# A decode step on one core: the first weight transfer issued as two, 16 partitions and then 112

## The chip, the core and the metric

The kernel runs on one core of a Trainium2 chip. The metric is device time in microseconds (us) for one launch, from the first instruction to the end of the last one. Before the change three timed runs gave 1314.3, 1315.67 and 1316.89 us, so the median is 1315.67 us. The engines are named as in the profile: PE multiplies matrices, DVE works on vectors, ACT on activations, POOL does a few small things at the start, and SP issues nearly all the transfers from HBM (the memory of the chip) to SBUF (the memory of the core, 128 partitions).

## What is computed

One decoding step of a transformer block for two sequences (B = 2), one token each, D = 512, 32 heads of 128, a cache of 8192 positions, and a feed-forward layer of width 1792, all in float32:

```python
def _A_ref(x, k_cache, v_cache, wq, wo):
    q = (x @ wq).reshape(B, 1, 32, 128).transpose(0, 2, 1, 3)
    scores = einsum("bhqd,bhkd->bhqk", q, k_cache) * (128 ** -0.5)
    p = softmax(scores)
    o = einsum("bhqk,bhkd->bhqd", p, v_cache)
    return o.transpose(0, 2, 1, 3).reshape(B, 1, 4096) @ wo

h  = x + _A_ref(layernorm(x), k_cache, v_cache, wq, wo)
h2 = h + (silu(layernorm(h) @ w_gate) * (layernorm(h) @ w_up)) @ w_down
```

The two caches are 2 x 32 x 8192 x 128 floats each, 268.4 MB apiece. The weight `wq` is 512 x 4096 floats, 8.39 MB. Every byte is used once.

## The kernel before, in words

SBUF holds three large areas of 64 KB per partition, A, B and C. Keys of the units alternate between A (`kA`) and B (`kB`). The values (`vC`) always go to C, and so do `wq` at the very start (`wqC`) and the last weight, `w_down` (`wdC`), at the end. A unit is two heads of one sequence: 128 partitions by 16384 floats, 8.39 MB of keys and as much of values. There are 32 units.

All large loads pass through the helper `load` (line 131), which issues one transfer on SP and lets it add 16 to a semaphore when it has landed. SP issues them in the order of the program, and the transfers of SP form one queue (q1 in the profile) on the core's 16 DMA engines. The order at the start is `wq`, the keys of unit 0 in two halves (`k0`, `k0b`), the keys of unit 1 (`kB`), then the values of unit 0. Before the values SP waits until the matmuls that read `wq` are done, since both lie in area C:

```python
if u == 0:
    sp.wait_ge(s["pe"].h, 3)
else:
    sp.wait_ge(s["pv"].h, u)
```

From there on SP issues the values of unit u when PE is through with those of the unit before, and the keys of unit u+2 when DVE has summed up those of unit u (`red`).

`wq` is laid out so that partition p holds rows 4p to 4p+3 of the matrix, which is one contiguous piece of 64 KB in HBM per partition. The input `x` comes by a small transfer of its own on ACT's queue. While `wq` is on its way DVE, POOL and PE normalize `x` and turn it (`xT`). PE then waits for `wq` and for `xT` (the two waits ahead of line 256), multiplies (line 261), ACT copies the result (line 270), PE spreads it over the partitions (line 281), and ACT writes `q_all` (line 291). With the first piece of `q_all` and `k0`, DVE begins the scores of unit 0: products (line 302) and sums (line 308).

For each unit DVE then takes the maximum (337, 340), PE and ACT do the softmax (393 to 401, 352 to 356), PE multiplies with the values (408) in a loop, and the output is gathered (371, 420). After the last unit come the output projection, the second normalization and the feed-forward layer, whose last load is `wdC`; lines 535 to 569 work on it, and the result is written by two small transfers.

Of the kernel before, what the change touches and what calls it, by code (L numbers as in the profile page):

```python
# [9 lines left out]
P = 128  # L10
# [35 lines left out]
def decode_block(nc, x, k_cache, v_cache, wq, wo, w_gate, w_up, w_down, out):  # L46
# [10 lines left out]
    sp, pe, act, dve, pool = nc.sync, nc.tensor, nc.scalar, nc.vector, nc.gpsimd  # L57

    def arena(name, at, shape):
        return nc.alloc_sbuf_tensor_at(name, list(shape), F32, offset=at)  # L60
# [4 lines left out]
    wq_s = arena("wqC", C, [P, DC, H * DH])  # L65
# [5 lines left out]
    m = Map(nc, BASE + 3 * SLOT, nc.sbuf_usable_end)  # L71
# [46 lines left out]
    s = {n: Count(nc, f"s_{n}") for n in names}  # L118
# [11 lines left out]
    def load(c, dst, src):  # L130
        c.on(sp.dma_start(dst, src), 16)
# [4 lines left out]
    flat = lambda t, a, b: t[:, a:b, :].rearrange("p j d -> p (j d)")  # L136

    s["x"].on(act.dma_start(xs[:, :], x.rearrange("b s d -> (b s) d")), 16)
    load(s["wq"], wq_s[:, :, :], wq.rearrange("(p c) m -> p c m", p=P))
    half = NJ // 2  # L140
    for name, j0 in (("k0", 0), ("k0b", half)):
        load(
# [108 lines left out]
    sel_done = s["dve"].n  # L251


    pe.wait_ge(s["wq"].h, 16)
    pe.wait_ge(s["dve"].h, xT_done)
    rows = (wide0, wide1)
    for r in range(2):
# [380 lines left out]
```

## Time and profile before

| | |
|---|---|
| median of three runs | 1315.67 us |
| time of the profiled execution | 1314.05 us |
| its span, first to last instruction | 1312.3 us |
| DVE busy | 1130.5 us, 86% |
| PE busy | 425.3 us, 32% |
| bytes read from HBM | 564.66 MB |
| queue q1, share of the 16 DMA engines' time | 99.4% |

The span is what the page's shares refer to; the profiled execution took 1.75 us more than it, which is what lies around it. The share of a queue is the time that its packets took, summed over the 16 DMA engines, over 16 times the span. In the views by windows a packet is counted whole where it starts, so windows of a few microseconds scatter.

### The profile page before, as it was taken

The numbers are of one execution on the slowest core, as the hardware profiler recorded it, in microseconds if no ns is written. First come the engines' busy times: TensorE is split into PE (matmuls) and PEld (weight loads), VectorE is DVE, ScalarE is ACT, GpSimd is POOL, SyncE is SP. The second block draws the span as 40 slices with busy tenths as digits, with TensorE's granted clock in tenths as the row PEclk, the third lists the DMA queues.
The fourth block names the chain that finished last, engine by engine and source line by source line (L and its number), as shares of the span: only waits on it lengthen the run. The fifth ranks groups of instructions, "written<-read, shape, count | busy, mean of one in ns | idle before, by whom it ended". The sixth has DMA issues, their size and how long they took to land. (4 is left out here: it accounts for less than half of the span.)

```text
span 1312.3 us, 6527 instructions
## 1 busy us (share of the span) xinstructions
PE 425.3 (32%) x2844; PEld 142.8 (11%) x2844; DVE 1130.5 (86%) x191; ACT 75.7 (6%) x242; POOL 1.8 (0%) x8
## 2 busy tenths in 40 slices
PE   3233223332322333322333332233332123333267
PEld 0110001110001111000111000011100011101012
DVE  1999998889888889988888998888898888899831
ACT  0100000000000000000000000000000000000010
POOL 0000000000000000000000000000000000000000
PEclk9665566666556666655666655666665566665578
DMA  9999999999999999999999999999999999999997
GB/s 408 450 422 443 419 443 419 443 440 427 439 423 443 431 435 439 423 441 421 445 439 425 439 423 443 437 429 440 423 441 427 439 442 423 439 423 439 443 419 313
DMA packets 10540, 564.77 MB, mean 430 GB/s; under 512 B 1178, under 2 KB 1186, under 8 KB 1444
## 3 DMA queue, kind: packets, MB, share of 16 engines
q1 hardware_dynamic: 10520, 564.66, 99.4%
q8 instruction: 4, 0.07, 0.0%
q14 instruction: 4, 0.03, 0.0%
q10 hardware_dynamic: 12, 0.01, 0.0%
HBM read 564.66 MB, written 0.00 MB: 430 GB/s over the span
## 5 line engine op out<-in xcount | busy, mean ns | idle before, releaser
L408 PE MATMUL bank<-vC,p 128*8 128x512 f32 x2048 | 291.8, 734 | 584.9 <-PEq L121 584.9
L302 DVE TENSOR_TENSOR kA<-kA,q_all 128x16384 f32<-128x16384 f32 (+1 forms) x17 | 275.7, 16220 | 64.3 <-DMA kA<-in_A_k_cache_dram 36.9
L302 DVE TENSOR_TENSOR kB<-kB,q_all 128x16384 f32<-128x16384 f32 x16 | 275.6, 17223 | 39.6 <-DMA kB<-in_A_k_cache_dram 39.6
L308 DVE TENSOR_REDUCE s<-kA 128x128 f32<-128x16384 f32 (+1 forms) x17 | 275.7, 16216 | 0.1
L308 DVE TENSOR_REDUCE s<-kB 128x128 f32<-128x16384 f32 x16 | 275.5, 17220 | 0.0
L408 PEld LDWEIGHTS bank<-vC,p 128*8 128x8 f32 x2048 | 60.5, 103 | 790.1 <-issue 790.1
L393 PE MATMUL bank<-ident,m 128*1 128x128 f32 x64 | 18.7, 395 | 182.9 <-PEq L121 182.9
L371 ACT ACTIVATE osb<-bank,r 128x512 f32<-128x512 f32 x32 | 22.0, 687 | 902.0 <-PE bank L408 902.0
L420 PE MATMUL bank<-sel,osb 128*128 128x2 f32 x256 | 32.8, 250 | 29.0 <-PEq L121 29.0
L420 PEld LDWEIGHTS bank<-sel,osb 128*128 128x128 f32 x256 | 31.0, 191 | 57.7 <-issue 57.7
L401 PE MATMUL bank<-rs,hm 128*128 128x1 f32 x64 | 17.9, 348 | 44.1 <-PEq L121 44.1
L340 DVE TENSOR_REDUCE gm<-bank 1x2 f32<-1x128 f32 x32 | 8.9, 278 | 24.6 <-PE bank L393 24.6
L356 ACT ACTIVATE p<-s,nb 64x128 f32<-64x128 f32 x64 | 25.9, 405 | 1.4
L199 DVE BATCH_NORM_STATS2 stats<-bank 2x6 f32<-2x512 f32 x1 | 0.7, 686 | 28.7 <-PE bank L460 28.7
L393 PEld LDWEIGHTS bank<-ident,m 128*1 128x1 f32 x64 | 3.6, 80 | 185.1 <-issue 185.1
L397 PE MATMUL bank<-gm,nscale 1*128 1x2 f32 x64 | 17.6, 343 | 14.8 <-PEq L121 14.8
L401 PEld LDWEIGHTS bank<-rs,hm 128*128 128x128 f32 x64 | 16.1, 312 | 46.0 <-issue 46.0
L397 PEld LDWEIGHTS bank<-gm,nscale 1*128 1x128 f32 x64 | 15.8, 305 | 29.9 <-issue 29.9
L352 ACT ACTIVATE nb<-bank 128x2 f32<-128x2 f32 x32 | 5.5, 172 | 228.2 <-PE bank L397 228.2
L261 PE MATMUL bank<-wqC,xT 128*32 128x512 f32 x64 | 9.1, 732 | 16.4 <-DMA wqC<-in_A_wq_dram 16.4
L356 ACT ACTIVATION_READ_ACCUMULATOR p<-s,nb 64x1 f32 x64 | 11.8, 185 | 0.0
L337 DVE TENSOR_REDUCE m<-s 128x1 f32<-128x128 f32 x32 | 9.2, 286 | 1.1
(71 smaller groups left out, 87.3 us busy)
## 6 DMA issues: line engine op xcount, KB each, us to landing
kA<-in_A_k_cache_dram SPq DMA_DIRECT2D x2, 4096.0 KB, 36.3
vC<-in_A_v_cache_dram SPq DMA_DIRECT2D x1, 6144.0 KB, 24.7
wgB<-in_B_w_gate_dram SPq DMA_DIRECT2D x1, 3584.0 KB, 31.9
wdC<-in_B_w_down_dram SPq DMA_DIRECT2D x1, 3328.0 KB, 20.8
wuB<-in_B_w_up_dram SPq DMA_DIRECT2D x1, 2688.0 KB, 37.9
vC<-in_A_v_cache_dram SPq DMA_DIRECT2D x1, 2048.0 KB, 29.2
wuB<-in_B_w_up_dram SPq DMA_DIRECT2D x1, 896.0 KB, 39.6
vC<-in_A_v_cache_dram SPq DMA_DIRECT2D x31, 29.3
```

The source lines that it names most:

```text
L261: ins = pe.matmul(rows[r][32 * t : 32 * t + 32, :], xT[:, c, :], wq_s[:, c, n0 : n0 + 512], start=(c == 0), stop=(c == DC - 1),)
L302: dve.tensor_tensor(kt, kt, q_all[:, u, :][:, None, :].to_broadcast([P, n, DH]), op=OP.mult)
L308: return dve.tensor_reduce(s_t[:, j0 : j0 + n], ks[u % 2][:, j0 : j0 + n, :], axis=AX.X, op=OP.add)
L337: s["mt"].on(dve.tensor_reduce(m_t[:, :], s_t[:, :], axis=AX.X, op=OP.max))
L340: dve.tensor_reduce(gm[:, :], small1[0:1, :P].rearrange("p (e q) -> p e q", e=2), axis=AX.X, op=OP.max,)
L356: ins = act.activation(p2[a:z, :, e], s_t[a:z, :], AF.Exp, bias=nb[a:z, e : e + 1], scale=SCALE, accum_out=rs[a:z, :],)
L371: act.activation(osb[:, :, :].rearrange("p j d -> p (j d)"), opart[:, :], AF.Copy, scale=r_t[:, :],)
L393: pe.matmul(small1[0:1, :P], m_t[:, :], ident[:, :], start=True, stop=True).then_inc(s["mrow"].h, 1)
L397: pe.matmul(small1[:, 264:266], nscale[:, :], gm[:, :], start=True, stop=True).then_inc(s["nbp"].h, 1)
L401: pe.matmul(small1[:, 256:257], hm[:, :], rs[:, :], start=True, stop=True).then_inc(s["den"].h, 1)
L408: ins = pe.matmul(opart[32 * t : 32 * t + 8, :], p2[:, 4 * g : 4 * g + 4, :].rearrange("p j b -> p (j b)"), vs[:, 4 * g : 4 * g + 4, :].re ...
L420: ins = pe.matmul(small2[:, 16:18], osb[:, j, :], sel8[:, j, :], start=(j == 0), stop=(j == 3))
```

## The change

The transfer of `wq` is issued as two, one behind the other, on the same queue: the first to partitions 0 to 15 (1.05 MB), the second to partitions 16 to 127 (7.34 MB). Both add 16 to the same semaphore, and PE now waits for 32. On both sides the four rows of a partition are named as one run of 16384 floats. Bytes, destination, and everything after it in the program are as they were.

```diff
     s["x"].on(act.dma_start(xs[:, :], x.rearrange("b s d -> (b s) d")), 16)
-    load(s["wq"], wq_s[:, :, :], wq.rearrange("(p c) m -> p c m", p=P))
+    wq_src = wq.rearrange("(p c) m -> p (c m)", p=P)
+    for a, z in ((0, 16), (16, P)):
+        load(s["wq"], wq_s[a:z, :, :].rearrange("p c m -> p (c m)"), wq_src[a:z, :])
     half = NJ // 2
@@
-    pe.wait_ge(s["wq"].h, 16)
+    pe.wait_ge(s["wq"].h, 32)
     pe.wait_ge(s["dve"].h, xT_done)
```

On SP, at the start of the program, the transfers stood in this order before (`wqC` is `wq` in area C, the numbers are partitions by floats):

```order
L131 DMA wqC<-in_A_wq_dram 128x16384
L131 DMA kA<-in_A_k_cache_dram 128x8192 x2
L131 DMA kB<-in_A_k_cache_dram 128x16384
L131 DMA vC<-in_A_v_cache_dram 128x16384
L131 DMA kA<-in_A_k_cache_dram 128x16384
```

They now stand so:

```order
L131 DMA wqC<-in_A_wq_dram 16x16384
L131 DMA wqC<-in_A_wq_dram 112x16384
L131 DMA kA<-in_A_k_cache_dram 128x8192 x2
L131 DMA kB<-in_A_k_cache_dram 128x16384
L131 DMA vC<-in_A_v_cache_dram 128x16384
```

One transfer became two of 16 and 112 partitions; all the others keep their shapes and their order. On PE, DVE, ACT and POOL the rows are the same as before.

## The prediction, made before the changed kernel was run

> **What bounds the kernel now.** I read the page's slices and its queues first, then the chain of waits, then the first 100 us in order of time.
>
> ```profile
> DMA  9999999999999999999999999999999999999997
> q1 hardware_dynamic: 10520, 564.66, 99.4%
> HBM read 564.66 MB, written 0.00 MB: 430 GB/s over the span
> ```
>
> The DMA engines are busy in every slice but the end of the last. DVE with 86% is busy too, but the queue of transfers never runs dry, and the bytes set the time. The queue's row gives the pace of one DMA engine: 564.66 MB / (0.994 x 16 x 1312.3 us) = 27.06 GB/s. So the 64 KB that one partition of `wq` takes occupy one engine for 65,536 B / 27.06 GB/s = 2.42 us. I call this time T and work with it below.
>
> ```profile
> by line: DMA wdC<-in_B_w_down_dram 1.6%; PE bank L408 0.7%; PE bank L535 0.3%; DVE ysb L544 0.0%; PE bank L550 0.0%; issue 0.0%; DVE res L569 0.0%; PE bank L560 0.0%
> ...
> 1284.12 20.79 DMA wdC<-in_B_w_down_dram
> 1304.91 0.14 issue
> 1305.04 3.63 PE bank L535 x52
> ```
>
> The chain of waits ends in the last load, which lands at 1304.91 us, and 7.4 us of computing follow. With every engine full from the start to there, a delay of any one DMA engine at the start is still there at 1304.91 unless something later gives it slack. What could give slack is the moment when the queue is empty. For that I read SP, DVE and PE in order of time:
>
> ```profile
> 0.74 0.39 SPq L131 DMA_DIRECT2D wqC<-in_A_wq_dram  x1
> 1.20 0.89 SPq L131 DMA_DIRECT2D kA<-in_A_k_cache_dram  x2
> 2.12 0.53 SPq L131 DMA_DIRECT2D kB<-in_A_k_cache_dram  x1
> ...
> 6.32 0.17 DVE L229 COPY xT<-bank 128x8 f32<-128x8 f32 x1 [0.73 <-PE bank L222]
> ...
> 22.67 9.10 PE L261 MATMUL bank<-wqC,xT 128*32 128x512 f32 x64 [16.38 <-DMA wqC<-in_A_wq_dram]
> ...
> 31.84 0.33 SPq L131 DMA_DIRECT2D vC<-in_A_v_cache_dram  x1
> ...
> 34.34 8.69 DVE L302 TENSOR_TENSOR kA<-kA,q_all 128x8192 f32<-128x8192 f32 x1 [27.40 <-ACT q_all L291]
> ```
> ```profile
> 69.10 0.33 SPq L131 DMA_DIRECT2D kA<-in_A_k_cache_dram  x1
> ```
>
> `wq` has landed at about 22.6 us. Behind it lie 16.8 MB of keys, 16T = 38.7 us of work, to about 61.3 us. The values of unit 0 are issued at 31.84, 29 us before the queue would need them, and last to about 80.7 us; the next keys are issued at 69.10, 11.6 us ahead. So the stock behind `wq` is never empty. Everything that these issues wait for (the `wq` matmuls, then `q_all`, then DVE's sums of unit 0) itself starts when `wq` lands. Move the landing by d and the issues move by d, and so does the queue: the stock stays what it is, and d reaches the end of the kernel. It isn't used up by idle time, since there is none.
>
> **The change part by part.** First the small parts. *One more issue on SP* is one more row like the 0.39 us one at 0.74. It pushes the issue of the keys from 1.20 to about 1.6 us; cover is the `wq` transfer, which keeps the engines until about 22.6. Cost 0, and 0.4 us if the cover were gone. *The wait for 32* is one instruction as before; it ends when the later of the two transfers has landed. Behind it on PE are the 64 matmuls of line 261, and for these wait ACT, DVE and SP's first values, as just counted. `xT` (6.49 us) is there long before. *The merged dimensions* leave one run of 64 KB per partition: 0.
>
> *An earlier start* would be a gain. The only row that bounds it is the landing of `wq`:
>
> ```profile
> wqC<-in_A_wq_dram SPq DMA_DIRECT2D x1, 21.9
> ```
>
> Of these 21.9 us, 8T = 19.4 us are bytes (128 partitions over 16 engines are 8T each), so at most 2.5 us go to starting and finishing. A first transfer of 16 partitions may get its descriptions to the engines sooner than one of 128. Part of the 2.5 us must be latency that any transfer has: the bounds are 0 and 2.5 us, and I take 0.5, nearer the low end because two issues now stand where one did.
>
> *The split itself* is the large term, and the trace has no row for a big transfer to fewer than 128 partitions. Every large one writes all 128 evenly, so its rows fit two pictures. In picture A the 27.06 GB/s belong to each DMA engine wherever it writes. Then 16 partitions are 1T for each engine, 112 are 7T, and the sum is 8T as before: cost 0. In picture B they belong to places: 128 partitions in 16 groups of 8, each group taking 27.06 GB/s, and engines that meet in a group share it. As long as a transfer covers all groups evenly one can't see the difference. Under B the cost of the first transfer depends on how many groups 16 neighbouring partitions reach. If they reach all 16 it is 1T, if they all lie behind one it is 16T = 38.7 us. Between ends so far apart I take the geometric middle, 4 groups: 4T = 9.7 us, where 1T would have done.
>
> The Trainium skill bears on this. "SBUF — State Buffer", section "Door 1: The DMA port swizzle", says that DMA bandwidth depends on how many of 16 SBUF ports the partitions of a transfer reach, and its table gives partitions 0 to 15 four ports and 104 GB/s at 1 MiB. By that figure the first transfer would be an estimated 10.1 us, and picture A would be out. No run here has shown it so far. "DMA: Bandwidth & Descriptors", section "Rules for kernel authors", also says of two transfers to disjoint partition halves not to bother, and to use one of 128 partitions.
>
> Under B the second transfer costs as well. Each engine has 7 partitions to write, 7T if engines never meet in a group, 14T if each always meets one other. In a transfer of 128 the engines can each have a group to themselves; with 7 neighbours each, cut at partitions 16, 23, 30 and so on, they straddle groups of 4 or 8 and must meet some of the time. I take the middle, 10.5T = 25.4 us. What counts is the slowest engine, not the mean, because the semaphore waits for all of them and because nothing later evens the queue out: engines that got through early run ahead into the keys, and then wait for issues that hang on the slow one.
>
> The sum under B: 4T + 10.5T = 14.5T instead of 8T, so +6.5T = +15.7 us, bounds 4T + 7T - 8T = +3T = +7.3 us and 4T + 14T - 8T = +10T = +24.2 us. Less 0.5 us for the start it is +15.2. The profiled execution's 1314.05 us (span 1312.3 and 1.75 around it) becomes 1329.2 us; it lies 1.62 us below the median of the runs, so the median becomes **1330.8 us**, from 1322.5 to 1339.4 by the bounds.
>
> **The rivals.** *Not slower: the start alone.* If picture A holds, the only thing left is the earlier start. Its place is the 2.5 us between issue and landing that aren't bytes, its price 0 to -2.5 us, and it decides as soon as 16 partitions take the engines no more than 1T + 0.2T. The time is 1313.2 to 1315.7 us, with my 0.5 us 1315.2. For it speaks that no row shows engines sharing anything; against it, that all rows are of the one even shape, so they couldn't show it.
>
> *Much slower: partitions dealt out in turn.* Under B, if engine e gets partitions 16+e, 32+e and so on instead of seven neighbours, all 16 engines are always in 16 neighbouring partitions, and each of the 8 rounds costs 4T instead of 1T: 32T - 8T = +24T = +58.1 us, 1373.3 us less the start. Against it: engines that drift apart would no longer meet, so even then it should come out below that.
>
> *Fewer engines.* Under A, the 112 partitions might go to fewer than 16 engines, with 8 engines 14 each: 1T + 14T - 8T = +7T = +16.9 us, 1332 us. That would look like my forecast in time; the share of the DMA engines in the first 40 us tells them apart, since under B the engines are slow but occupied, and here half of them go ahead to the keys. A split into 14 engines with 8 each would be only +1T, 2.4 us. 7 partitions on each of 16 come out even, so I hold this for unlikely.
>
> **How the numbers follow.** About 0.2% (2.6 us) is what a measurement of this kernel can tell from no change. Chances: picture B with neighbours 0.62, picture A with the start alone 0.20, dealt out in turn 0.08, fewer engines 0.10. I put B over A because any unevenness costs the whole kernel its slowest engine and only perfect independence costs nothing, and because one pace in all slices, for rows of 64 KB, for halves of 32 KB and for weights alike, is what an even share of the places would give as well. All of B, the deal in turn and fewer engines are slower by over 0.2%: 0.80. Of A's 0.20, 0.03 goes to faster, as it takes the whole 2.5 us and a little scatter, and 0.17 to within 0.2%. The likeliest case's own range is 1322.5 to 1339.4. The range for 8 in 10 goes down to 1314.8, into the case of no change, and up to 1341.0, which leaves out the deal in turn and A's best half.
>
> **What would show it.** In the changed profile the 16-partition transfer's time from issue to landing: some 11 to 12 us under B, under 5 us under A. Then the start of the matmuls of line 263 (261 before): 22.67 us before, about 38 us under B, 22 us under A. The first slice's 408 GB/s would fall by the delay's share of 32.8 us, to between 220 and 350, the other slices stay at 420 to 450, and the wait for DVE's first products grows by the same 15 us. The last load lands later by what the matmuls started later. If the matmuls start late and the end doesn't move, there was slack that I haven't seen, and the step from landing to end is wrong. If the first transfer lands early and the second late, the first term is wrong and the second has the cause.

## The result, and the profile after

The changed kernel takes 1334.82 us (median of five runs, 1333.91 to 1336.03) against 1315.67 us (five runs, 1313.74 to 1316.89): a ratio of 1.0154, 95% interval 1.0141 to 1.0166. By the medians it is 19.15 us more for the same bytes (their quotient is 1.0146, inside the interval).

The slices of the page, first GB/s before, then the share of the DMA engines and GB/s after (40 slices, 33.4 us each after):

```profile
GB/s 408 450 422 443 419 443 419 443 440 427 439 423 443 431 435 439 423 441 421 445 439 425 439 423 443 437 429 440 423 441 427 439 442 423 439 423 439 443 419 313
```
```profile
DMA  9999999999999999999999999999999999999996
GB/s 216 376 437 432 426 432 440 440 433 428 432 436 440 432 434 428 434 440 434 432 430 432 440 436 436 430 430 434 440 436 432 428 433 438 438 432 430 432 429 288
```

The loss is in the first two slices. The last slice is lower as well, 288 after 313, because in this profile the computing behind the last load took longer, as shown below. In the row of busy shares the loss can't be seen: the engines show 9 tenths and more while they move 216 GB/s, half of what they moved before.

The packets in the two traces, which the views don't list one by one, show where the time goes. Each partition of `wq` is one packet of 64 KB. Before the change 16 packets were under way at once, as many as there are engines, and each took 2.42 us (up to 3.3 us in the first round). After it the 16 packets of the first transfer run side by side and take 7.7 to 9.1 us each. The 112 of the second follow in 16 rows of seven, one behind the other, and take 2.8 to 6.3 us each, 4.6 us in the median. The share of the DMA engines is 0.97 over the first 45 us, at 222 GB/s: a packet that is held up counts as busy.

The same start in order of time after the change, from the timeline, and the view of the tile `wqC`:

```profile
0.74 0.87 SPq L131 DMA_DIRECT2D wqC<-in_A_wq_dram  x2
1.65 1.11 SPq L131 DMA_DIRECT2D kA<-in_A_k_cache_dram  x2
...
6.32 0.17 DVE L231 COPY xT<-bank 128x8 f32<-128x8 f32 x1 [0.73 <-PE bank L224]
...
44.06 9.71 PE L263 MATMUL bank<-wqC,xT 128*32 128x512 f32 x64 [37.78 <-DMA wqC<-in_A_wq_dram]
...
53.84 0.33 SPq L131 DMA_DIRECT2D vC<-in_A_v_cache_dram  x1
...
56.33 8.69 DVE L304 TENSOR_TENSOR kA<-kA,q_all 128x8192 f32<-128x8192 f32 x1 [49.40 <-ACT q_all L293]
```
```profile
DMA to landing us min/median/max: 12.2/27.5/42.8
```

The 16 partitions land 12.2 us after their issue, the other 112 after 42.8 us, where all 128 had taken 21.9. PE waits 37.78 us for `wq` instead of 16.38, and the matmuls, the issue of the first values and DVE's first products all come 21 to 22 us later (22.67 to 44.06, 31.84 to 53.84, 34.34 to 56.33).

The chain of waits ends in the same load as before:

```profile
1303.69 20.78 DMA wdC<-in_B_w_down_dram
1324.48 0.14 issue
1324.61 5.99 PE bank L537 x52
```

It lands at 1324.48 us, 19.57 us later than before (1304.91). The profiled executions are further apart than that, 1314.05 and 1336.03 us, because the matmuls behind the load took 3.63 us in the one and 5.99 in the other. The windows behind the last load (PE busy, its granted clock after POOL) show why, before and after:

```profile
1304.91:1312.30 7.39, 4.23 (x68) 2.79 (x68) 0.72 (x2) 0.38 (x1) 0.00 (x0) 1.00 0.00 1
```
```profile
1324.48:1334.20 9.72, 6.60 (x68) 3.41 (x68) 0.72 (x2) 0.38 (x1) 0.00 (x0) 0.75 0.00 1
```

The granted clock was 1.00 there in one execution and 0.75 in the other. The change isn't what sets it: of the kernels below, the two that start without a delay (the split by columns and every second partition) have 3.65 and 5.31 us at this place in their profiles, and two that start about as late as the changed kernel (the other order and the halves) 3.65 and 3.63.

### The profile page after: what moved, and what is told of

The parts are those of the page before. It is cut to its first block, busy times and chain, and to the rows that moved or that the text cites. A ratio compares the mean times of both kernels' runs of the same rounds, so it can differ in the third digit from the quotient of the medians.

```text
span 1334.2 us, 6528 instructions
## 1 busy us (share of the span) xinstructions
PE 428.3 (32%) x2844; PEld 143.8 (11%) x2844; DVE 1130.4 (85%) x191; ACT 75.7 (6%) x242; POOL 1.8 (0%) x8
## 5 line engine op out<-in xcount | busy, mean ns | idle before, releaser
L422 PE MATMUL bank<-sel,osb 128*128 128x2 f32 x256 | 32.8, 250 | 28.9 <-PEq L121 28.9
```

The source lines that it names most:

```text
L422: ins = pe.matmul(small2[:, 16:18], osb[:, j, :], sel8[:, j, :], start=(j == 0), stop=(j == 3))
```

## The experiments

The edits of the split by columns, the other order and the two kinds of halves are shown against the changed kernel, the others against the kernel before. Each timed kernel ran 4 or 10 times beside 13 runs of the kernel before, from which the second time in each pair comes. The two kernels of loads alone, which are the kernel before with these loads put ahead of it, ran once each, for their traces.

**The same split by columns.** Two transfers of the same sizes, but each to all 128 partitions.

```diff
-    for a, z in ((0, 16), (16, P)):
-        load(s["wq"], wq_s[a:z, :, :].rearrange("p c m -> p (c m)"), wq_src[a:z, :])
+    wq_dst = wq_s[:, :, :].rearrange("p c m -> p (c m)")
+    for a, z in ((0, 2048), (2048, 16384)):
+        load(s["wq"], wq_dst[:, a:z], wq_src[:, a:z])
```

> wq is again issued as two transfers of 1.05 MB and 7.34 MB, but each goes to all 128 partitions (the first 2048 floats of a partition, then the other 14336). Theory B (partitions share places of one pace): both transfers cover all places evenly, so the cost is gone: 1315.7 us within 2.6, wq matmuls start at about 22.7 us. Rival (it costs to have two transfers, or a short one ahead of a long one): the cost stays, about +19 us, 1335.

Measured: 1314.49 us against 1315.55, ratio 0.9998 (0.9988 to 1.0007). The transfers of this kernel by size, and the start of the matmuls:

```profile
wqC<-in_A_wq_dram SPq DMA_DIRECT2D x1, 7168.0 KB, 21.0
wqC<-in_A_wq_dram SPq DMA_DIRECT2D x1, 1024.0 KB, 4.6
```
```profile
22.24 8.50 PE L264 MATMUL bank<-wqC,xT 128*32 128x512 f32 x64 [15.96 <-DMA wqC<-in_A_wq_dram]
```

1 MB to 128 partitions lands after 4.6 us, to 16 partitions after 12.2. Being two, and being a short one ahead of a long one, costs nothing that these runs can tell. The matmuls even start 0.43 us sooner than before, which is the size of the earlier start that the prediction allowed for, but the kernel as a whole doesn't tell it from no change.

**The delay alone.** `wq` loaded once more ahead of everything, into area B. The keys of unit 1 go to the same area, so SP waits for the extra load before it issues them.

```diff
+    wq_x = arena("wqX", BB, [P, DC, H * DH])
+    load(s["wqx"], wq_x[:, :, :], wq.rearrange("(p c) m -> p c m", p=P))
     load(s["wq"], wq_s[:, :, :], wq.rearrange("(p c) m -> p c m", p=P))
...
+    sp.wait_ge(s["wqx"].h, 16)
     load(s["kB"], flat(ks[1], 0, NJ), kv_src(k_cache, 1))
```

> The kernel before with wq loaded once more ahead of everything, to 128 partitions in area B, as pure delay: 8T = 19.4 us more on every DMA engine. If a delay of the queue at the start reaches the end whole, the kernel takes 1335.1 us (+19.4). If the stock of issued transfers or idle time later takes some of it up, it is less: under +10 us.

Measured: 1334.35 us, ratio 1.0149 (1.0132 to 1.0166), +18.8 us by the medians. In the profile the matmuls of `wq` start 19.53 us later than before, and the matmuls behind the last load (line 535 before, 538 here) 19.37:

```profile
42.20 9.70 PE L264 MATMUL bank<-wqC,xT 128*32 128x512 f32 x64 [35.92 <-DMA wqC<-in_A_wq_dram]
```
```profile
1324.41 3.63 PE bank L538 x52
```

So a delay that is the same on all engines at the start reaches the end whole. This step of the prediction had only been argued; here it is shown for such a delay.

**Ten kinds of loads, alone.** Each load is waited for before the next is issued, so the distance from one row's start to the next, halved, is the time of one.

```diff
...
+    probes = (
+        ("fourNear", 0, 4, 1), ("fourFours", 0, 13, 4), ("fourFar", 0, 97, 32),
+        ("sixteenNear", 0, 16, 1), ("sixteenFours", 0, 61, 4), ("sixteenEights", 0, 121, 8),
+        ("halfNear", 0, 64, 1), ("halfTwos", 0, 127, 2),
+        ("restNear", 16, 128, 1), ("allRows", 0, 128, 1),
+    )
+    for name, a, z, step in probes:
+        t = arena(name, C, [P, DC * H * DH])
+        for _ in range(2):
+            load(s["wqx"], t[a:z:step, :], wq_src[a:z:step, :])
+            sp.wait_ge(s["wqx"].h, s["wqx"].n)
```

> The kernel before with ten kinds of loads ahead of it, each twice and each waited for before the next is issued, 64 KB to a partition, into the same area. T = 2.42 us, and 2.5 us of start and end as with wq before. Theory B with places of four neighbours and four partitions 32 further on: 4 neighbouring partitions (fourNear) 4T + 2.5 = 12.2 us, 4 partitions in steps of 4 (fourFours) 1T + 2.5 = 4.9 us, 4 in steps of 32 (fourFar) 2T + 2.5 = 7.3 us; 16 neighbours 12.2, 16 in steps of 4 or of 8 7.3; 64 neighbours 8T + 2.5 = 21.9; 64 in steps of 2 between 4T and 8T, 12.2 to 21.9; 112 neighbours from partition 16 on 8T at least, as in the changed kernel about 13T + 2.5 = 34; 128 21.9. Rival (the number of partitions sets the pace, or any transfer of other than 128 is slow): the three kinds of 4 alike, the three kinds of 16 alike. Picture A (engines alone): 4 and 16 partitions all 4.9, 64 12.2, 112 19.4, 128 21.9.

SP in order of time (start, time from the first issue to the end of the second):

```profile
0.74 11.79 SPq L131 DMA_DIRECT2D fourNear<-in_A_wq_dram  x2
23.96 5.88 SPq L131 DMA_DIRECT2D fourFours<-in_A_wq_dram  x2
34.41 7.77 SPq L131 DMA_DIRECT2D fourFar<-in_A_wq_dram  x2
48.56 12.01 SPq L131 DMA_DIRECT2D sixteenNear<-in_A_wq_dram  x2
71.87 8.11 SPq L131 DMA_DIRECT2D sixteenFours<-in_A_wq_dram  x2
86.93 8.21 SPq L131 DMA_DIRECT2D sixteenEights<-in_A_wq_dram  x2
102.24 23.58 SPq L131 DMA_DIRECT2D halfNear<-in_A_wq_dram  x2
148.43 13.07 SPq L131 DMA_DIRECT2D halfTwos<-in_A_wq_dram  x2
173.70 33.10 SPq L131 DMA_DIRECT2D restNear<-in_A_wq_dram  x2
239.26 22.31 SPq L131 DMA_DIRECT2D allRows<-in_A_wq_dram  x2
283.06 0.33 SPq L131 DMA_DIRECT2D wqC<-in_A_wq_dram  x1
```

| partitions | us for one | less 2.5 us, in T = 2.42 us | theory B |
|---|---|---|---|
| 4 neighbours | 11.6 | 3.8 | 4 |
| 4, every fourth | 5.2 | 1.1 | 1 |
| 4, every 32nd | 7.1 | 1.9 | 2 |
| 16 neighbours | 11.7 | 3.8 | 4 |
| 16, every fourth | 7.5 | 2.1 | 2 |
| 16, every eighth | 7.7 | 2.1 | 2 |
| 64 neighbours (0 to 63) | 23.1 | 8.5 | 8 |
| 64, every second | 12.6 | 4.2 | 4 to 8 |
| 112 (16 to 127) | 32.8 | 12.5 | 8 or more |
| 128 | 21.9 | 8.0 | 8 |

The three kinds of four move the same 256 KB, and differ only in which partitions they write and, with them, which rows of `wq` they read: 11.6, 5.2 and 7.1 us. Sixteen neighbours take no longer than four. The rival of the number of partitions had the three kinds alike, and picture A had 4 and 16 partitions all at 4.9 us; both fall. The packets agree: four neighbours are four packets at once of 8.1 to 8.9 us each, every fourth partition four packets at once of 2.5 to 3.4 us, and 16 neighbours 16 packets at once of 8.3 to 8.9 us. The layout that fits is four neighbouring partitions to a place, and the four that lie 32 further on in the same place. It is the layout that the Trainium skill gives in "SBUF — State Buffer", section "Door 1: The DMA port swizzle", for its 16 ports. That section of the Trainium skill has 104 GB/s for partitions 0 to 15 at 1 MiB; the 1.05 MB here make 90 GB/s over the whole 11.7 us and 114 GB/s over the 9.2 us without start and end.

That the place is in SBUF and not on the side of HBM is argued, not shown: no run reads the same rows into other partitions. Against HBM speaks the end of the kernel before. If a place were a stretch of 256 KB in HBM, four rows of 64 KB, then pieces of 28 KB to a partition, as `w_gate` has them, would share such stretches in another way, nine to one, and the deal to the engines that is even for `wq` would be uneven for `w_gate`. Yet its 128 packets take 1.06 us each, which is the full pace of 27 GB/s again.

**The other order.** The 112 partitions first.

```diff
-    for a, z in ((0, 16), (16, P)):
+    for a, z in ((16, P), (0, 16)):
```

> The same two transfers in the other order, 112 partitions first and then 16. Theory B: what each transfer costs is set by its partitions, not by its turn, so wq again takes some 17T to land and the kernel comes to 1330 to 1337 us. Rival (the order makes the cost, because a small transfer at the head leaves the engines out of step for the large one): the delay shrinks to that of 16 partitions alone, +7.3 us or less, under 1324 us.

Measured: 1335.74 us, ratio 1.0164 (1.0147 to 1.0181). The matmuls start here:

```profile
44.60 9.49 PE L263 MATMUL bank<-wqC,xT 128*32 128x512 f32 x64 [38.32 <-DMA wqC<-in_A_wq_dram]
```

44.60 us against 44.06 with the 16 first: the turn makes 0.5 us at most, the partitions make the rest.

**Two halves, of neighbours and of every second partition.** Number, sizes and order of the transfers are the same in both kernels.

```diff
-    for a, z in ((0, 16), (16, P)):
+    for a, z in ((0, 64), (64, P)):
```

> wq in two transfers of 64 partitions, 0 to 63 and 64 to 127. In the probe 64 neighbours took 23.1 us each alone, 20.6 us without the 2.5 us of start and end: 8.5T where an even share is 4T. Theory B: 2 x 20.6 = 41.2 us instead of 19.4, so +21.8 at the landing of wq; what overlaps where one ends and the other begins can only lessen it, at most to 8T = +0, since the two halves reach different places: between 1325 and 1337 us. Rival (only an odd count such as 112 or a short first transfer costs): 1315.7.

```diff
-    for a, z in ((0, 16), (16, P)):
-        load(s["wq"], wq_s[a:z, :, :].rearrange("p c m -> p (c m)"), wq_src[a:z, :])
+    wq_dst = wq_s[:, :, :].rearrange("p c m -> p (c m)")
+    for a, z in ((0, 127), (1, 128)):
+        load(s["wq"], wq_dst[a:z:2, :], wq_src[a:z:2, :])
```

> The same as the halves in number, size and order of transfers, but the first takes the 64 even partitions and the second the 64 odd ones. In the probe 64 partitions in steps of 2 took 12.6 us alone, 10.1 without start and end, 4.2T. Theory B: 2 x 4.2T = 8.4T for 8T, +0.8 us, 1316.5 us within 2.6. Rival (64 partitions are slow as such): as slow as the halves.

Measured: the halves 1335.24 us against 1314.45, ratio 1.0170 (1.0139 to 1.0201; three of the four runs lie between 1335.10 and 1335.24, the fourth at 1342.46); every second partition 1316.07 us, ratio 1.0005 (0.9995 to 1.0015). The matmuls, first of the halves, then of every second:

```profile
44.17 8.95 PE L263 MATMUL bank<-wqC,xT 128*32 128x512 f32 x64 [37.88 <-DMA wqC<-in_A_wq_dram]
```
```profile
23.04 8.50 PE L264 MATMUL bank<-wqC,xT 128*32 128x512 f32 x64 [16.76 <-DMA wqC<-in_A_wq_dram]
```

This pair is the plainest: 44.17 or 23.04 us for the same two transfers of 64 partitions, depending on which 64. Behind the first round of 16, the packets of the halves take 4.9 to 5.1 us each, those of every second partition 2.42. The halves' +21.5 us at the matmuls is 2 x 20.6 - 19.4 = 21.8 with almost nothing overlapping. "Don't bother" with disjoint halves, as the Trainium skill has it in "DMA: Bandwidth & Descriptors", section "Rules for kernel authors", holds here: two halves of neighbours cost 21.5 us, and two of every second partition gain nothing. The Trainium skill also says, in "SBUF — State Buffer", section "Can I just issue two DMAs to hit both halves?", that only one transfer spanning all 128 partitions reaches all 16 ports. Read as every partition in one transfer, that doesn't hold here: 64 partitions, every second, moved 4.19 MB in 10.1 us, 415 GB/s, in the probe.

**The 16 partitions alone.** The kernel before, with `wq`'s first 16 partitions loaded once more ahead of it into area B.

```diff
+    wq_x = arena("wqX", BB, [P, DC * H * DH])
+    load(s["wqx"], wq_x[0:16, :], wq.rearrange("(p c) m -> p (c m)", p=P)[0:16, :])
     load(s["wq"], wq_s[:, :, :], wq.rearrange("(p c) m -> p c m", p=P))
...
+    sp.wait_ge(s["wqx"].h, 16)
     load(s["kB"], flat(ks[1], 0, NJ), kv_src(k_cache, 1))
```

> The kernel before with one more transfer ahead of wq: its partitions 0 to 15 (1.05 MB) into area B, as pure delay. Theory B: 4T = 9.7 us (9.2 in the probe) on the engines ahead of an undisturbed wq, so 1325.0 us. Picture A, where only bytes count: 1T = 2.4 us, 1318.0 us.

Measured: 1324.08 us against 1314.45, ratio 1.0065 (1.0048 to 1.0081): +9.6 us by the medians, and 9.3 us at the start of the matmuls in the profile (31.96), for 1 MB that would take 1T = 2.4 us when spread evenly.

```profile
wqX<-in_A_wq_dram SPq DMA_DIRECT2D x1, 12.1
wqC<-in_A_wq_dram SPq DMA_DIRECT2D x1, 30.7
```

**Where the 112's time comes from.** More loads alone, in the same manner.

```diff
...
+    probes = (
+        ("rest", 16, 128), ("restLow", 0, 112), ("ninetysix", 32, 128),
+        ("eighty", 48, 128), ("upperHalf", 64, 128), ("fortyeight", 16, 64),
+    )
```

> More loads alone, 64 KB to a partition, each twice. What of the 12.5T of partitions 16 to 127 is the uneven load on the places (8T, as no place holds more than 8 partitions) and what comes from engines that meet? In time from issue to issue, 2.5 us of it start and end: if it is the load of the fullest place alone, all of 16 to 127, 0 to 111, 32 to 127, 48 to 127 and 64 to 127 take 8T + 2.5 = 21.9 us or a little over, and 16 to 63 too (8 partitions in each of four places). If meeting adds to it because 112 isn't a multiple of 32, then 112 stays at 32 us in both positions, 96 and 64 come to 22 to 23 us, and 80 and 48 lie above their 8T.

```profile
0.74 33.98 SPq L131 DMA_DIRECT2D rest<-in_A_wq_dram  x2
68.09 32.72 SPq L131 DMA_DIRECT2D restLow<-in_A_wq_dram  x2
133.31 32.15 SPq L131 DMA_DIRECT2D ninetysix<-in_A_wq_dram  x2
197.43 27.45 SPq L131 DMA_DIRECT2D eighty<-in_A_wq_dram  x2
251.63 23.32 SPq L131 DMA_DIRECT2D upperHalf<-in_A_wq_dram  x2
297.41 26.77 SPq L131 DMA_DIRECT2D fortyeight<-in_A_wq_dram  x2
350.69 0.35 SPq L131 DMA_DIRECT2D wqC<-in_A_wq_dram  x1
```

Halved, in us: 33.7, 32.6, 32.1, 27.1, 22.9 and 26.6; less 2.5 and in T: 12.9, 12.5, 12.2, 10.2, 8.4 and 10.0. In each of them the fullest place holds 8 partitions, so an uneven load alone would give 8T throughout. Only the half of 64 is near it. The others take 2T to 5T more, and not because 112 isn't a multiple of 32: 96 partitions take 12.2T. That part of the expectation was wrong. The packets point to engines that meet, round after round: the 96 partitions go in six rounds of 16 packets, and behind the first round each packet takes 4.7 to 5.1 us, twice the 2.42 of a packet in the even loads.

A working that fits: let each of 16 engines take its share of neighbouring partitions in order (3, 5, 6 or 7 of them), all in step, and let each step last as long as the fullest place in it. With the layout of the first probe that gives 9T for 16 to 63, 10T for 48 to 127, 12T for 32 to 127 and 14T for the 112, against 10.0, 10.2, 12.2 and 12.5 to 12.9. It doesn't fit 128, or 64 in steps of two, for which it gives 16T and 8T where 8.0 and 4.2 were measured; there the shares must be dealt in another way. The packets confirm the number of rounds (3, 5, 6 and 7), but not which engine wrote which partition, which neither the views nor the packets tell; so this stays a fit and is not shown.

## Why the prediction was right, point by point

**The bound and the way to the end.** Right for a delay that is the same on all engines: the queue is full, and 19.5 us come out as 19.4 at the end. Not quite for the uneven one: in the changed kernel 21.4 us at the matmuls become 19.6 at the last load, so 1.8 us didn't arrive, where the prediction let the delay reach the end whole. The halves lose 0.6 us on this way and the other order 0.8. Both kernels have packets of queue q8 (`instruction`, 16 KB each) on one of the engines. In the packets of the trace before, one of these takes 0.96 us at about 38 us, and from there on the 16 engines finish a transfer up to 1.84 us apart instead of 0.75; after the change they stay 2.2 us apart without such a jump. If the packet hit the last engine in the one case and an earlier one in the other, that is 1.0 us of the difference. This was not tested, and the cause stays open.

**The small parts.** Right. The added issue and the wait for 32 cost nothing that shows: with the split by columns, which has both, the ratio is 0.9998. The earlier start was put at 0.5 us; by columns the matmuls start 0.43 us sooner, though with 16 partitions this is buried.

**4T for the first transfer.** Right: 3.8T in the probe, and 9.6 us added to the kernel by such a transfer alone where 9.7 was the price. The mechanism was reasoned, but the size came out by luck: in the sum the number 4 is a geometric middle between 1 and 16, with no row behind it. That the places are fours of neighbours with 32 between them was first borne out by the probe.

**10.5T for the second.** The term that was mis-sized. Inside its bounds of 7T and 14T it measured 12.5T to 12.9T alone. The lower bound couldn't be reached by the picture's own count: when 16 partitions lie in four places, the other twelve still have all their 8 to take, so 8T is the least. With 3.8T ahead of it that makes 16.3T to 16.7T instead of 14.5T for the sum, 4 to 5 us more at the landing of `wq`. The middle was too kind: in the changed kernel none of the 112 packets got through in 2.42 us, and half of them took 4.6 us or more, so engines meet in every step. The 0.5 us of an earlier start didn't show either. So the matmuls started at 44 us, not at about 38, and the first slice fell to 216 GB/s, just under the 220 to 350 that was given; the second slice, which was to stay above 420, fell to 376, since the delay reaches past 33 us.

**The sum.** +15.2 us was forecast, +19.15 measured, in the range from 1322.5 to 1339.4 that belonged to this case. The forecast is 6 us short at the matmuls and only 4 us short at the end, because of the 1.8 us that got lost on the way. The start that is only quicker, the rival on the other side, is out by the three kinds of four; so are fewer engines, since four packets at once take 5.2 or 11.6 us by their place alone, and 16 packets are under way throughout the two transfers of the changed kernel. Partitions dealt out in turn would have made some 58 us by the prediction's count, with packets of about 4T = 9.7 us; the longest of the 112 took 6.3.

## What to carry to other kernels

In these runs the transfers from HBM into SBUF that had the full pace were those whose partitions lie evenly over all 128. Beside the bytes it counts how many partitions share the fullest place, and whether the engines meet there. If such a load has to be split, split it along the row, or take every second partition, rather than cut off a block of neighbours. In a kernel whose queue is never empty, a slow transfer at the start costs nearly its whole excess at the end (19.6 of 21.4 us here), and the busy share of the DMA engines hides it: read GB/s beside it.

## What the runs showed of the hardware that was not expected

Sixteen engines writing to 16 neighbouring partitions need as long as four engines writing to four of them (11.7 and 11.6 us), so here the pace goes by the places and not by the number of engines: four engines share a place in both. A load of 96 of 128 partitions takes 32.1 us where all 128 take 21.9: less data, half as long again. The 112 packets of the second transfer were under way for 31.7 us with all engines shown as busy. And the 52 matmuls behind the last load took 3.63 us or 5.3 to 6.0 us from one profile to the next, with a granted clock of 1.00 or 0.75 in the two profiles shown above, which is most of the difference between the profiled executions' 22.0 us and the medians' 19.15.
